# Block products for the first batch's second layer, 64-row value products in early pairs, and a new hand-written order, in a fused attention and feed-forward kernel

## The chip, the cores and the metric

The kernel runs on one core of a Trainium2 chip. The core has TensorE (PE, matrix products into PSUM), VectorE (DVE), ScalarE (ACT), GpSimd (POOL) and SyncE (SP, which here only issues DMAs). The metric is the time of one execution in device microseconds; less is better.

## The reference: what is computed

Cosine attention for 8 batches, 12 heads, 448 positions and 64 dimensions, followed by a feed-forward layer of 768 to 2048 to 768 on all 3584 positions:

```
q_n = q / (norm(q) + 1e-6);  k_n = k / (norm(k) + 1e-6)
attn = softmax(q_n @ k_n.T / tau);  x = attn @ v          # heads side by side: 768 wide
h = x @ w_in;  g = h * clip(h + 3, 0, 6) / 6;  out = g @ w_out
```

Inputs and output are float32; the products run on bf16.

## The kernel before, in words

**Pairs.** The two heads g = 0 and 1 of a batch that are 6 apart are worked on together as one pair; there are HP = 6 pairs in a batch and NP = 48 in all. Items are the query or key halves of two pairs: item j is loaded by `load_qk` (LQ, on SP's queue) into one of the buffers `raws` inside the large tile `big`, squared (`square`, SQ, on DVE, ACT or POOL as its second argument v, a or p says), summed by a DVE `reduce` (RE), turned into inverse norms on ACT (`norms`, NO; with "v" the last steps on DVE), multiplied (`normalise`, NM) and transposed, on PE (`transposes`, TR) in the early items and by DMA (`crossbar`, XD) from item 14 on. `copy_q`, `copy_k`, `copy_k3` (CQ, CK, CS) bring the transposed halves to where the scores read them.

**Attention.** The keys of a pair are taken in four groups: three with 128 keys of each head and a fourth, "M", with the last 64 keys of both heads in one tile, head A in rows 0 to 63 and head B in rows 64 to 127. `scores` (SC, L435 and L438) multiplies keys by queries, mostly in 64 rows of PE, since a head has 64 dimensions; `exps` (EX, L456) exponentiates on ACT; `values` (VA, L478) multiplies by the values, eight matmuls of 65 columns for each group, into the PSUM tile `PV`; the 65th column gives the softmax's sum. `finish_values` (FI) divides on DVE. `back` (BK) or a DMA (`back_crossbar` XB, `back_two` XP) and `copy_x` (CX) make x transposed. In group M the value tile `vx` has zero rows where the other head's keys are, so that 128 rows can be used; from pair FIRST = 18 on the matmuls take only the 64 rows of their own head.

**Feed-forward.** `mm1_unit` (L583) makes 128 of the 2048 hidden values for one batch, in six matmuls of 448 columns, one for each pair of the batch; ACT (`relu`) and DVE (`product`) make g from them. For the second product, positions are taken in tiles of 128; batch 0 has tiles 0 to 2, and its last 64 positions join batch 1. From batch 1 on, tiles are taken in pairs (`PAIRS`) and the product of two tiles with `w_out` is done by seven block products of 8 matmuls (`product_unit`, L756; numbered 1 to 7) from sums of blocks of g (`g_sum`, L734) and of `w_out` (`weight_sums`, L705). The sums y3 and y4 replace blocks of `w_out` in place. ACT copies the products 3, 4, 5 and 2, DVE adds into 1, 6 and 7, POOL makes the three additions of `both` and `rest`. Product 5 goes on in the bank of 3, and 2 in that of 4, once ACT has copied those. A tile without a partner is done by `single_unit` (L836): two units of 16 matmuls, with the sum "e" of g, because `w_out` has been changed. Batch 0 is done by `mm2_unit` (L630) on the unchanged `w_out`, six units of 16 matmuls.

**The order.** Each engine does its instructions in the order in which the program names them. Up to pair 17 that order is written out by hand, token by token, in `PLAN`: the name of an operation, its numbers and its engine. U takes the next unit of `stream` (first products "1" and second products "2", in the sequence `ORDER`); UA and UV do the next waiting finishing step on ACT or DVE. DP.n puts n filler matmuls of zeros (L938, 248 columns) on PE, D.n the same with 512 columns (L933); they keep PE running where it has nothing to do yet. W issues the next weight DMA from POOL's queue, WS is a weight sum, GL copies the 64 leftover positions of a batch. From pair 18 on a loop names the operations; `units`, `TURNS` and `side` say which products and sums go with which pair. Transposed tiles, scores and units share six PSUM banks in turn (`next_bank`) once the start's own banks are closed (OPEN); an operation that gets a bank waits for the reader of its last content.

Of the kernel before, what the change touches and what calls it, by code (L numbers as in the profile page):

```python
# [17 lines left out]
FIRST = 18  # L18
ORDER = "111111111111111111111111111111222222"

PLAN = [
# [42 lines left out]
def kernel(  # L64
# [72 lines left out]
    def raw_before(j):  # L137

        return j - NR if j < 26 else j - NR + 2

    def raw_buffer(j):
        return raws[j % NR if j < 26 else (j - 26) % (NR - 2)]
# [326 lines left out]
    def values(i, g):  # L469
# [4 lines left out]
        for n, name in enumerate(GROUPS[g]):  # L474
            for j in range(4):
                for h in (range(2) if name == "M" else ["AB".index(name[0])]):
                    rows = slice(64 * h, 64 * h + 64) if name == "M" and i >= FIRST else slice(0, 128)
                    nc.tensor.matmul(  # L478
                        pv_out(j, h),
                        at[rows, n, q_cols(i // HP, j)],  # L480
                        vt[rows, 3 + h if name == "M" else 5 * h + int(name[1]), :],
                        start=(name in ("A0", "B0") and j == 0),
                        stop=last,
                        skip_group_check=True,
                    )
# [57 lines left out]
    evac_n = [0]  # L543
# [33 lines left out]
    def mm1_unit(b, fc):  # L577
        needs(*(("CX", i) for i in range(b * HP, (b + 1) * HP)))
        assert len(weights) <= 10 - 2 * (4 * fc // FCN)
        x, g, c0 = xT[b % 2], g_of(b), b % 2 * SR  # L580
        ps, key = bank_of(None, 1)
        for cc in range(CC):
# [3 lines left out]
                x[:, cc, 0:S],  # L586
                start=(cc == 0),
                stop=(cc == CC - 1),
            )
        def relu():  # L590
# [32 lines left out]
    def mm2_unit(b, t, m):  # L623
        assert not weights and ("y4", "y3")[m] not in [x for x, _ in summed]
        complete(b, t)
        g = g_of(b)
        ps, key = bank_of(None, 1)
        cols = slice(m * MH, m * MH + MH)
        for fc in range(FCN):
            nc.tensor.matmul(  # L630
                ps[:, 0:MH],
                g[:, fc, g_cols(b, t)],
                w_out_sb[:, fc, cols],
                start=(fc == 0),
                stop=(fc == FCN - 1),
            )

        def store():
            o = out_tile()
            if on_act:  # L640
                nc.scalar.copy(out=o[:, :], in_=ps[:, 0:MH])
            else:
                nc.vector.tensor_copy(out=o[:, :], in_=ps[:, 0:MH])
            unread[key] = 0
            result(b, t, cols, o)

        evac_n[0] += 1
        on_act = evac_n[0] % 2 == 1
        post["a" if on_act else "v"].append(store)

# [3 lines left out]
    def second(b):  # L654
        assert b % 2 == 0
        return [(mm2_unit, b, t, m) for m in (1, 0) for t in range(3)]
# [7 lines left out]
    PAIRS = [p for b in range(0, B, 2) for p in (((b, 0), (b, 1)), ((b + 1, 3), (b + 1, 0)), ((b + 1, 1), (b + 1, 2)))][1:]  # L664
# [10 lines left out]
    wide_late = [tail(c, MH) for c in range(TAIL, TAIL + 2 * (len(PAIRS) - LOOP) * MH, MH)]  # L675

    def sum_of(n, what):
# [3 lines left out]
        if n < LOOP or n == len(PAIRS) - 1:  # L681
            return gs[what + str(n % 2) if what == "7" else what]
        return late_sums[n % 2][what]

    def d_and_e(n):
        if n < LOOP:
            return wide[n % 2], wide[2]
# [427 lines left out]
```

## Time and profile before

| What | us |
|---|---|
| Median of 3 runs (lowest to highest) | 403.25 (402.74 to 404.51) |
| The profiled execution's own time | 403.12 |
| Its span, from the first to the last instruction | 401.3 |
| PE busy | 393.5 |
| DVE busy | 288.7 |
| ACT busy | 275.4 |
| POOL busy | 238.4 |

The mean granted clock of TensorE was 0.999 of full speed. The span is what the profile divides by; the time of an execution is 1.8 us longer. A line of a group names the source line, engine, operation, output and inputs, then how often it stands and how long one takes. Matmuls are pipelined: one shown with 326 ns lets the next one start after about 160.

### The profile page before, as it was taken

To read this page: it belongs to the slowest core of one execution; us is meant where nothing else is said; L and a number is where in the kernel's file an instruction comes from. 1 tells how busy PE (TensorE), PEld (TensorE's weight loads), DVE (VectorE), ACT (ScalarE), POOL (GpSimd) and SP (SyncE) were. 2 spreads that over 40 slices of the span, in tenths; PEclk is the share of its full clock that TensorE was granted. 3 is DMA by queue.
4 is the path that set the end of the run, shared out by engine and by line. 5 is a ranking of instruction groups with operands and counts; after the bars stand their busy time and mean duration, and the time that the engine had idled before them with its cause. 6 is when DMAs were issued, how large, how long until landed. Compare 5 with 4: busy or idle time off the path is not lost.

```text
span 401.3 us, 9620 instructions
## 1 busy us (share of the span) xinstructions
PE 393.5 (98%) x3691; PEld 235.1 (59%) x3691; DVE 288.7 (72%) x521; ACT 275.4 (69%) x600; POOL 238.4 (59%) x230
## 2 busy tenths in 40 slices
PE   7999999999999999999999999999999999999996
PEld 5666556556665556555555556555555556555563
DVE  7898968779768877677867887697656566644663
ACT  5899889978467687777858769668648755235230
POOL 7799858772554987588475966857665500500070
PEclk9999999999999999999999999999999999999999
DMA  8999999995869559684889658985863423140134
GB/s 289 312 234 238 170 205 280 192 231 143 194 136 238 113 144 207 168 231 110 194 193 204 157 130 158 175 192 140 185 158 71 106 46 68 31 89 20 28 72 99
DMA packets 93166, 63.75 MB, mean 159 GB/s; under 512 B 56128, under 2 KB 93120, under 8 KB 93120
## 3 DMA queue, kind: packets, MB, share of 16 engines
q1 hardware_dynamic: 87408, 56.45, 60.1%
q0 software_dynamic: 5312, 6.29, 9.5%
q8 instruction: 29, 0.48, 0.5%
q10 hardware_dynamic: 400, 0.39, 0.3%
q14 instruction: 17, 0.14, 0.1%
HBM read 45.61 MB, written 11.01 MB: 141 GB/s over the span
## 4 chain that ended last, share of the span: by engine, by line
PE 94%; ACT 3%; DVE 2%; issue 0%
PE M L583 26%; PE M L756 17%; PE PV L478 12%; PE M L438 5%; PE Y L583 5%; PE Z L583 5%; PE Y L756 5%; PE Z L756 4%; PE M L630 3%; PE M L836 3%; ACT at L456 2%; PE PV L938 2%; PE Z L438 2%; PE Y L438 1%; PE Z L836 1%; PE Y L630 1%
## 5 line engine op out<-in xcount | busy, mean ns | idle before, releaser
L583 PE MATMUL M<-xT,w_in_sb 128*128 128x448 bf16 x540 | 113.8, 352 | 0.0
L583 PEld LDWEIGHTS <-w_in_sb 128*128 128x128 bf16 x768 | 72.1, 98 | 63.6 <-issue 3.0
L456 ACT ACTIVATE at<-M 128x448 bf16<-128x448 f32 x193 | 96.2, 568 | 19.0 <-PE Y L438 9.8
L289 POOL TENSOR_TENSOR nrm<-big,r 128x896 bf16<-128x896 f32 (+1 forms) x46 | 76.4, 1666 | 8.1 <-ACT r L279 3.0
L230 POOL TENSOR_TENSOR big<-big 128x896 f32<-128x896 f32 (+4 forms) x46 | 71.8, 1564 | 14.3 <-DMA big<-in_k_dram 6.2
L598 DVE SCALAR_TENSOR_TENSOR gT<-u,M 128x448 bf16<-128x448 bf16 x80 | 49.5, 618 | 38.3 <-ACT u L592 37.6
L592 ACT ACTIVATE u<-M,bias 128x448 bf16<-128x448 f32 x90 | 58.8, 653 | 25.7 <-PE M L583 25.0
L478 PEld LDWEIGHTS <-at 128*128 128x128 bf16 (+1 forms) x1536 | 54.2, 97 | 20.2 <-issue 11.8
L478 PE MATMUL PV<-vx,at 128*128 128x65 bf16 (+1 forms) x1536 | 62.9, 193 | 0.0
L395 POOL COPY km<-tT 64x128 bf16<-64x128 bf16 x34 | 14.7, 433 | 67.0 <-DMA tT<-nrm 35.1
L242 DVE TENSOR_REDUCE n<-big 128x14 f32<-128x896 f32 (+1 forms) x50 | 51.6, 1041 | 0.7 <-POOL big L230 0.4
L785 POOL TENSOR_TENSOR big<-big 128x384 f32<-128x384 f32 x11 | 11.9, 1084 | 54.5 <-ACT big L804 54.4
L756 PEld LDWEIGHTS <-gT 128*128 128x128 bf16 x288 | 27.9, 98 | 19.6
L499 DVE TENSOR_TENSOR on<-PV,rc 128x512 bf16<-128x512 f32 x48 | 33.2, 692 | 1.7
L456 ACT ACTIVATE at<-Z 128x448 bf16<-128x448 f32 x52 | 29.3, 563 | 4.4 <-PE Z L438 2.3
L756 PE MATMUL M<-w_out_sb,gT 128*128 128x384 bf16 x176 | 32.2, 326 | 0.0
L438 PE MATMUL M<-tT,kz 64*128 64x448 bf16 (+1 forms) x173 | 31.5, 351 | 0.3 <-ACT at L456 0.3
L456 ACT ACTIVATE at<-Y 128x448 bf16<-128x448 f32 x49 | 27.7, 565 | 5.7 <-PE Z L438 5.7
L756 PEld LDWEIGHTS <-gs 128*128 128x128 bf16 x224 | 21.5, 98 | 14.7 <-DVE gs L734 0.3
L308 POOL CAST vx<-big 128x512 bf16<-128x512 f32 x37 | 27.5, 748 | 0.8 <-DMA big<-in_v_dram 0.7
L756 PE MATMUL M<-w_sum,gs 128*128 128x384 bf16 (+1 forms) x160 | 27.7, 318 | 0.0
L583 PE MATMUL Y<-xT,w_in_sb 128*128 128x448 bf16 x114 | 24.7, 352 | 0.0
(134 smaller groups left out, 565.9 us busy)
## 6 DMA issues: line engine op xcount, KB each, us to landing
big<-in_k_dram SPq DMA_DIRECT2D x24, 448.0 KB, 5.1
big<-in_q_dram SPq DMA_DIRECT2D x24, 448.0 KB, 4.3
out_dram<-o SPq DMA_DIRECT2D x107, 96.0 KB, 2.2
big<-in_v_dram SPq DMA_DIRECT2D x48, 128.0 KB, 4.5
big<-in_v_dram SPq DMA_DIRECT2D x48, 96.0 KB, 4.5
w_in_sb<-in_moe_w_in_dram POOLq DMA_DIRECT2D x8, 384.0 KB, 6.5
w_out_sb<-in_moe_w_out_dram POOLq DMA_DIRECT2D x4, 768.0 KB, 10.7
tT<-nrm SPq DMA_TRANSPOSE x34, 3.0
```

Of the source, the lines that this page charges most:

```text
L230: engines[e].tensor_tensor(out=o, in0=i, in1=i, op=ALU.mult)
L242: nc.vector.tensor_reduce(out=n2_and_r[0][:, d % 2, j % 2, c], in_=sq[:, :, :, :].rearrange("p g c d -> p (g c) d")[:, c, :], axis=AX.X, o ...
L289: engines[e].tensor_tensor(out=nrm[:, :, g, :].rearrange("p c g d -> p g c d"), in0=raw_of[j][:, g, :, :], in1=n2_and_r[2][:, d % 2, j % 2, :]
L308: (engines[e].copy if e == "a" else engines[e].tensor_copy)(out=o, in_=f)
L438: nc.tensor.matmul(o, ks, qt[rows], start=True, stop=True)
L456: nc.scalar.activation(out=o, in_=x, func=AF.Exp, scale=inv_tau)
L478: nc.tensor.matmul(pv_out(j, h), at[rows, n, q_cols(i // HP, j)], vt[rows, 3 + h if name == "M" else 5 * h + int(name[1]), :], start=(name ...
L499: nc.vector.tensor_tensor(out=on[:, :, :, :].rearrange("p j h d -> p h j d"), in0=pv4[:, :, :, 0:D], in1=rc[:, :, :].to_broadcast([128, 2, ...
L583: nc.tensor.matmul(ps[:, 0:S], w_in_sb[:, cc, fc * 128 : (fc + 1) * 128], x[:, cc, 0:S], start=(cc == 0), stop=(cc == CC - 1),)
L592: nc.scalar.activation(out=u[:, :], in_=ps[:, 0:S], func=AF.Relu, bias=half_bias, scale=1.0 / 6.0)
L598: nc.vector.scalar_tensor_tensor(out=g[:, fc, c0 : c0 + S], in0=u[:, :], scalar=1.0, in1=ps[:, 0:S], op0=ALU.min, op1=ALU.mult,)
L756: nc.tensor.matmul(m, lhs[:, c, :], rhs[:, c, c0 : c0 + width], start=(base is None and c == 0), stop=(c == KC - 1), skip_group_check=True,)
```

## The change

- Batch 0's tiles 0 and 1 become a pair of their own, numbered -1, done by seven block products in the sequence 3, 4, 5, 2, 1, 6, 7; tile 2 becomes a single (s0.0, s0.1). `mm2_unit` is gone. For it the plan names five sums of g (GS.6, 2, 7, 5, 1), the sum "e" for the single, two POOL steps (UP) and all of the weight sums; the last half of y4 leaves the loop's `side[18]`.
- `values` takes a third argument: with ".t" in the plan, group M of an early pair is done in 64 rows. Thirteen of the first 17 pairs have it: 0, 1, 3, 6, 7 and 9 to 16.
- The first four first products of batch 0 are cut into pieces of 2, 2 and 1 matmuls (UH), named as the transposed pairs become ready, and a rest that U does.
- The order of nearly all of `PLAN` is new: the first transposition stands behind 40 fillers where it stood behind 50, the second behind 53 where it was 60; fillers of 248 columns number 96 where they were 90, those of 512 columns 2 where it was 1. Squares, copies and casts go to other engines: 4 casts of values on DVE where there were 9, 4 on ACT where there were 2, 40 on POOL where there were 37. Item 20 is loaded later, into another buffer (`raw_buffer`).

The diff without the plan, cut to its core:

```diff
-ORDER = "111111111111111111111111111111222222"
+ORDER = "1" * 30 + "2" * 9
...
     def raw_buffer(j):
-        return raws[j % NR if j < 26 else (j - 26) % (NR - 2)]
+        return raws[5 if j == 20 else j % NR if j < 26 else (j - 26) % (NR - 2)]
...
-    def values(i, g):
+    def values(i, g, by_halves=None):
...
-                    rows = slice(64 * h, 64 * h + 64) if name == "M" and i >= FIRST else slice(0, 128)
+                    rows = slice(64 * h, 64 * h + 64) if name == "M" and (by_halves or i >= FIRST) else slice(0, 128)
...
+    CUTS = (0, 2, 4, 5)
+    open_units = {}
+
+    def mm1_piece(b, fc, c0, c1, bank=None):
+
+        needs(*(("CX", b * HP + c) for c in range(c0, c1)))
+        assert len(weights) <= 10 - 2 * (4 * fc // FCN)
+        if c0 == 0:
+            open_units[b, fc] = *bank_of(bank, 1), 0
+        ps, key, n = open_units[b, fc]
+        assert n == c0
+        for cc in range(c0, c1):
             nc.tensor.matmul(
                 ps[:, 0:S],
                 w_in_sb[:, cc, fc * 128 : (fc + 1) * 128],
-                x[:, cc, 0:S],
+                xT[b % 2][:, cc, 0:S],
                 start=(cc == 0),
                 stop=(cc == CC - 1),
+                skip_group_check=True,
             )
+        open_units[b, fc] = ps, key, c1
...
     def second(b):
-        assert b % 2 == 0
-        return [(mm2_unit, b, t, m) for m in (1, 0) for t in range(3)]
+        return products(" ".join(f"{x}.{b - 1}" for x in "3452167") + f" s{b}.0 s{b}.1")
...
-    PAIRS = [p for b in range(0, B, 2) for p in (((b, 0), (b, 1)), ((b + 1, 3), (b + 1, 0)), ((b + 1, 1), (b + 1, 2)))][1:]
+    PAIRS = dict(
+        enumerate((p for b in range(0, B, 2) for p in (((b, 0), (b, 1)), ((b + 1, 3), (b + 1, 0)), ((b + 1, 1), (b + 1, 2)))), -1)
+    )
...
     def d_and_e(n):
+        if n < 0:
+            return tuple(big[:, RAW + c : RAW + c + MH] for c in (0, MH))
...
     side = {
-        18: [(weight_sums, "y4", KC // 2, KC // 2)], 19: sums(0, "62"), 20: sums(0, "1"),
+        19: sums(0, "62"), 20: sums(0, "1"),
```

The part of the new plan around batch 0's second products (each line of the plan is a string):

```
"SC.15.1 U EX.15.0 EX.15.1 FI.13 VA.14.0 VA.14.1 VA.14.2 VA.14.3.t UV SC.15.2 U SC.15.3 WS.1.1 UA UA WS.6.1 UV",
"WS.y3.1 FI.14 LV.8 EX.15.2 WS.y3.0 XD.17 U U EX.15.3 UA VA.15.0 XP.12 WS.7.1 WS.y4.0 WS.y4.1 CS.16.v VC.18.a",
"LV.10 GS.5 GS.1 CK.17.a VA.15.1 CK.16.a VA.15.2 UA U U UA UA U UA U UV UV UV UP GL.0 XD.18 SC.16.0 VA.15.3.t",
```

More of the change, by code (lines that the diff above doesn't have):

```diff
@@ L137, in raw_before @@
     def raw_before(j):
-        return j - NR if j < 26 else j - NR + 2
+        return 19 if j == 20 else j - NR if j < 26 else j - NR + 2
     def raw_buffer(j):
-        return raws[j % NR if j < 26 else (j - 26) % (NR - 2)]
+        return raws[5 if j == 20 else j % NR if j < 26 else (j - 26) % (NR - 2)]
     sqs = [item(NR + i) for i in range(2)]
@@ L541, in back_two @@
             issued.update((("BK", x), ("CX", x)))
-    evac_n = [0]
     post = {"a": [], "v": [], "p": []}
@@ L575, in g_left @@
         left_done.add(b)
-    def mm1_unit(b, fc):
-        needs(*(("CX", i) for i in range(b * HP, (b + 1) * HP)))
+    CUTS = (0, 2, 4, 5)
+    open_units = {}
+    def mm1_piece(b, fc, c0, c1, bank=None):
+        needs(*(("CX", b * HP + c) for c in range(c0, c1)))
         assert len(weights) <= 10 - 2 * (4 * fc // FCN)
-        x, g, c0 = xT[b % 2], g_of(b), b % 2 * SR
-        ps, key = bank_of(None, 1)
-        for cc in range(CC):
+        if c0 == 0:
[3 more added lines that the diff above has]
+        for cc in range(c0, c1):
             nc.tensor.matmul(
@@ L585, in mm1_unit @@
                 w_in_sb[:, cc, fc * 128 : (fc + 1) * 128],
-                x[:, cc, 0:S],
+                xT[b % 2][:, cc, 0:S],
                 start=(cc == 0),
                 stop=(cc == CC - 1),
+                skip_group_check=True,
             )
+        open_units[b, fc] = ps, key, c1
+    def mm1_unit(b, fc):
+        mm1_piece(b, fc, open_units[b, fc][2] if (b, fc) in open_units else 0, CC)
+        ps, key, _ = open_units.pop((b, fc))
+        g, c0 = g_of(b), b % 2 * SR
         def relu():
@@ L621, in out_tile @@
         return sb.tile([128, MH], FP32, name="o", tag="o", bufs=4)
[L623 to L649, printed above, removed]
     def firsts(b, *fcs):
@@ L654, in second @@
     def second(b):
-        assert b % 2 == 0
-        return [(mm2_unit, b, t, m) for m in (1, 0) for t in range(3)]
+        return products(" ".join(f"{x}.{b - 1}" for x in "3452167") + f" s{b}.0 s{b}.1")
     LEFT, RIGHT = slice(0, MH), slice(MH, 2 * MH)
-    PAIRS = [p for b in range(0, B, 2) for p in (((b, 0), (b, 1)), ((b + 1, 3), (b + 1, 0)), ((b + 1, 1), (b + 1, 2)))][1:]
+    PAIRS = dict(
+        enumerate((p for b in range(0, B, 2) for p in (((b, 0), (b, 1)), ((b + 1, 3), (b + 1, 0)), ((b + 1, 1), (b + 1, 2)))), -1)
+    )
+    LAST = max(PAIRS)
     LOOP = 8
@@ L674 @@
     wide = [big[:, c : c + MH] for c in range(0, 3 * MH, MH)]
-    wide_late = [tail(c, MH) for c in range(TAIL, TAIL + 2 * (len(PAIRS) - LOOP) * MH, MH)]
+    wide_late = [tail(c, MH) for c in range(TAIL, TAIL + 2 * (LAST + 1 - LOOP) * MH, MH)]
     def sum_of(n, what):
@@ L680, in sum_of @@
             return gs["1"] if n < B - 2 else late_sums[1]["e"]
-        if n < LOOP or n == len(PAIRS) - 1:
+        if n < LOOP or n == LAST:
             return gs[what + str(n % 2) if what == "7" else what]
@@ L743, in product_unit @@
         base = None if apart else {"2": "4", "5": "3", "6": "1"}.get(name)
+        if n < 0:
+            needs(("NM", 13))
+            assert base is None or (n, base) in ready
         if base is None:
@@ L876 @@
     }
-    APART = {(n, y) for n in range(len(PAIRS)) for x, y in (("5a", "3"), ("2a", "4")) if f"{x}.{n}" in " ".join(TURNS.values()).split()}
+    APART = {(n, y) for n in PAIRS for x, y in (("5a", "3"), ("2a", "4")) if f"{x}.{n}" in " ".join(TURNS.values()).split()}
     side = {
-        18: [(weight_sums, "y4", KC // 2, KC // 2)], 19: sums(0, "62"), 20: sums(0, "1"),
+        19: sums(0, "62"), 20: sums(0, "1"),
         21: sums(1, "75"), 22: sums(1, "621"),
@@ L965 @@
         "NM": normalise, "VC": vcast, "TR": transposes, "XD": crossbar, "XB": back_crossbar, "XP": back_two, "CQ": copy_q, "CK": copy_k, "CS": copy_k3, "SC": scores,
-        "EX": exps, "VA": values, "FI": finish_values, "BK": back, "CX": copy_x, "U": unit, "UA": lambda: finish_units("a"), "UV": lambda: finish_units("v"),
+        "EX": exps, "VA": values, "FI": finish_values, "BK": back, "CX": copy_x, "U": unit, "UH": lambda n, k, bank=None: mm1_piece(0, n, CUTS[k], CUTS[k + 1], bank), "UA": lambda: finish_units("a"), "UV": lambda: finish_units("v"), "UP": lambda: finish_units("p"), "GS": lambda x, *n: g_sum(*((0, "e") if x == "e" else (-1, str(x)))),
         "GL": g_left, "WS": lambda x, *h: weight_sums(str(x), *((h[0] * KC // 2, KC // 2) if h else (0, KC))), "UU": whole_units, "D": busy, "DP": busy_pv, "OPEN": open_ring,
```

76 rows, old and new, of the table PLAN are left out of this document.

## The prediction, written before the changed kernel was run

> **What bounds the kernel now.** I read the page's busy rows first, then the waits of TensorE (PE), then the timelines of the start, then the stretches of 5 and 10 us.
>
> ```profile
> PE 393.5 (98%) x3691; PEld 235.1 (59%) x3691; DVE 288.7 (72%) x521; ACT 275.4 (69%) x600; POOL 238.4 (59%) x230
> ```
>
> PE is busy for 98% of the span and the other engines are far below it. Its waits:
>
> ```profile
> PE PV L938 <- DVE xT L986: 2.5, 1, 2.5
> PE SC L438 <- DVE tT L357: 0.5, 2, 0.4
> PE SC L438 <- ACT at L456: 0.3, 1, 0.3
> PE M L438 <- ACT at L456: 0.3, 1, 0.3
> ```
>
> Columns: total us, times, longest. So time is saved here almost only where PE's own instructions get fewer or shorter. Busy PE is not PE at its rate, however: a matmul's shown 326 ns overlaps the next one. I therefore use distances from start to start, from the chain in order of time and the PE timeline:
>
> ```profile
> 2.48 8.13 PE PV L938 x50
> 10.99 1.06 PE PV L938 x10
> 94.55 2.60 PE M L630 x16
> 118.52 1.30 PE M L756 x8
> 38.84 0.65 PE L478 MATMUL PV<-vx,at 128*128 128x65 bf16 x16
> 39.42 0.36 PE L438 MATMUL Y<-tT,kz 64*128 64x448 bf16 x1
> 120.96 0.63 PE L478 MATMUL PV<-vx,at 128*128 128x65 bf16 x16
> 121.43 0.35 PE L438 MATMUL Z<-tT,kz 64*128 64x448 bf16 x1
> 122.09 0.66 PE L478 MATMUL PV<-vx,at 128*128 128x65 bf16 x16
> 122.59 0.32 PE L756 MATMUL Z<-w_out_sb,gT 128*128 128x384 bf16 x1
> ```
>
> A second-product matmul of 384 columns takes 2.60/16 = 162 ns, in L630 and in L756 alike. A filler matmul (L938, 248 columns) takes 106 ns, after a slow start: the first 50 take 163 each. Sixteen value matmuls of full rows take 0.50 us before full-row work (122.09 to 122.59) and 0.58 before the scores, which use 64 rows (38.84 to 39.42): a change between 128 and 64 rows costs about 0.09. At 120.96 eight of the sixteen already are 64-row ones, and the scores start after 0.47: halving the rows of eight matmuls saves 0.58 - 0.47 = 0.11.
>
> The start is the one part that PE does not bound alone:
>
> ```profile
> 15.00:20.00 5.00, 4.84 (x67) 3.23 (x64) 4.83 (x12) 4.97 (x10) 3.96 (x4) 1.00 1.04 359
> 25.00:30.00 5.00, 4.72 (x86) 3.18 (x85) 4.90 (x12) 4.97 (x9) 5.00 (x5) 1.00 1.13 204
> 90.00:100.00 10.00, 10.00 (x114) 6.18 (x113) 9.07 (x14) 8.33 (x19) 2.48 (x3) 1.00 0.57 145
> ```
>
> Columns after the stretch: its length, PE, weight loads, DVE, ACT, POOL, granted clock. From 15 to 30 us ACT and DVE are as full as PE, and the fillers hide how much PE really has to do. From 90 to 100 DVE is nearly full, POOL is not.
>
> **The change, part by part.** The counts come from the two programs' orders, engine by engine.
>
> (1) Second products of batch 0: 6 tiles of 16 matmuls (96) become 7 block products of 8 and 2 singles of 16 (88). 8 x 0.162 = **-1.30 us** on PE.
>
> (2) Fillers: 90 become 96, and a second 512-column one (L933, next start 0.23 later) comes in: 6 x 0.106 + 0.23 = **+0.86**.
>
> (3) Thirteen early pairs take their last keys in 64 rows: 13 x 0.11 = **-1.46** (with 0.112). The order holds 153 changes of row mode where it held 145, so 8 x 0.096 (the same distances, 125 against 29 ns) = **+0.77**. The row for the saving is the late pairs' own, so I take it as it is; most of the 13 groups stand beside scores, which pay a change of mode anyway. The Trainium skill, TensorEngine Tiling (Array Packing), section Key Properties, says against this part that changing the tiling mode drains TensorE; the trace agrees (0.09 us each time). Rival (d) is what that rule would do at worst.
>
> PE's own rows: -1.30 + 0.86 - 1.46 + 0.77 = **-1.13**.
>
> (4) Batch 0's first products are cut into pieces of 2, 2 and 1 of their 6 matmuls. Same matmuls, no cost; they fill PE while the last transposes arrive.
>
> (5) The start. Against the sum of its rows, PE's starts lag 5.1 us at the first transposition (10.44: 2.5 of wait and the slow fillers) and 7.9 at 41 us: 2.8 us are lost there. 0.4 of it is the wait of the first scores on the DVE copy. In the new order ten fillers fewer stand before the first transposition and seven before the second, so PE and with it DVE's copy come earlier; adding DVE's rows up to that copy, it ends at about 12.3 us and PE arrives at 12.5, so I drop the 0.4. Then exps: they take 0.80 us for two banks and 0.42 for one, from start to start. Summing ACT's queue, squares, norm steps and copies at their rows included, from the first exps to those of pair 7 gives 26.6 us before and 26.7 after; PE's rows between the same scores give 25.4 and 26.0. So PE must wait for ACT 1.1 us before and 0.6 after: -0.5. DVE's queue, summed in the same way up to each pair's division, is 0.9 us late at worst before and on time after. I take **-0.9**; the bounds are -2.8 (all of the loss goes) and +1.1 (the new order costs further waits as long as all those for scores of before, 0.5 + 0.3 + 0.3).
>
> (6) What DVE must do earlier. All weight sums now stand before batch 0's products, where they stood beside and behind them, with five sums of g in between and a sixth before the singles. Rows of before: a half weight sum 0.87 to 0.95, a sum of g 0.68. Following DVE's queue from about 76 us of the span: 11 us of such sums and 10 of its usual work lie in the 21 us until product 4, so nothing is spare. y3 ends some 0.5 before product 3 needs it, y4 0.5 after product 4 could start. What is queued behind that waiting matmul on PE is all the rest, so it counts in full: **+0.7** with small waits of banks. Bounds: 0 (DVE has run ahead) and +3.5 (rival b, two lost sums).
>
> (7) Hidden: POOL gets 3 additions of 1.0 us, beside 2.5 us of work in 90:100, ACT two more copies of 0.48 in a stretch where it has 1.7 of 10 free; if that cover is gone, a product's bank comes free half a microsecond later. The load of item 20 (key or query half of pairs 20 and 21) moves on SP's queue from 69 to about 104 us, behind normalise 19; its transposition then waits on SP until about 115 us, with a few output DMAs behind it, and its scores come some 20 us later. The loop from pair 18 on is the same but for one weight sum less (0.95 to 1.35 of DVE); PE has no wait there now, so it gains nothing.
>
> Sum: -1.13 - 0.9 + 0.7 = -1.3. The profiled execution took 403.12 us (span 401.3 and 1.8 around it), 0.13 below the median of 403.25: **401.8 us**.
>
> **Rivals.**
>
> (a) The start loses its waits altogether and y4 is in time: -1.13 - 2.0 + 0 gives 400.0. For it: every queue I summed has more room in the new order. Against: ACT is still 0.6 us short, and DVE's sums are tight. From -0.9 less y4's wait on it passes the 0.5% line.
>
> (b) The sums under POOL: slower. A sum of g of 1,024 elements takes
>
> ```profile
> L734 DVE TENSOR_TENSOR gs<-gT x26: 679/682/2170, 120.8 to 339.0; 128x1024 bf16<-128x1024 bf16 x26
> ```
>
> so 0.68 mostly, but up to 2.17. The long ones (131.5, 147.3, 235.4 us and others) lie under a normalise or square of POOL, though some short ones do as well. In the new order the sums 6 and 2 of g and half of weight sum 7 stand where POOL's queue holds three normalises in a row (1.65 us each). Each can lose up to 1.5 us; DVE has nothing spare, so product 4 and the next division wait by so much. Two lost sums: 403.12 - 1.13 - 0.9 + 3.5 = 404.6. It is slower by 0.5% from three on: with 0.5 + 3 x 1.5 = 5.0 of wait it is 406.1. Against: later POOL is nearly empty in the new order (casts moved to ACT), so the y sums run free.
>
> (c) No gain: ACT alone sets the start, so fewer PE instructions there only become waits (the four 64-row groups before 41 us, 0.44, are worth nothing), and y4's wait stays: -1.13 + 0.44 + 0.7 = 0.0, 403.1. For it: ACT's 4.97 of 5.00. Against: the cheaper matmuls after 41 us, and all of part 1, lie where only PE is full.
>
> (d) The 64 rows do not pay, because each group pays two changes of row mode of its own: 13 x 2 x 0.096 = 2.5 against the 1.46 saved, +1.0 where part 3 had -0.7, so 403.5. The counted changes speak against it.
>
> **Chances.** A measurement of this kernel can tell about 0.5% (2.0 us) from no change. Forecast 401.8: 0.45, with 0.05 of it beyond the line of 401.2; (a) 0.28; (b) 0.14, of which 0.09 beyond 405.3; (c) 0.08; (d) 0.05. Faster by over 0.5%: 0.33; within 0.5%: 0.40 + 0.05 + 0.08 + 0.05 = 0.58; slower: 0.09. The range goes from (a) with the whole bound of part 5 (403.12 - 1.13 - 2.8 = 399.2) to (b) with two lost sums, 404.6.
>
> **What would show it.** Right: PE's first scores start without a wait on DVE, at about 12.5 us; the loop's first scores stand about 1.3 us earlier than before and the distance stays to the end; products of batch 0 take 1.30 per eight; a wait of PE of about 0.5 us in front of product 4 (the L751 line) on a DVE weight sum. Wrong: weight sums or sums of g on DVE that take over 1 us between 80 and 98 us (b), more waits on exps between 15 and 41 us (c), a value group of the last keys whose next start comes after 0.2 us (d).

## The result, and the profile after

The changed kernel takes 409.90 us (median of 6 runs, 409.55 to 411.46); the kernel before, beside it, took 403.74 (402.74 to 404.71). The ratio is 1.0169, with an interval of 1.0145 to 1.0193: slower, where 401.8 was forecast and 404.6 was the upper end of the range. The profiled execution took 409.8 us with a span of 407.8; its mean granted clock was 0.990.

The page's busy rows and its row of granted clock:

```profile
PE 394.7 (97%) x3690; PEld 233.4 (57%) x3690; DVE 295.5 (72%) x528; ACT 278.9 (68%) x604; POOL 236.5 (58%) x235
...
PEclk9999999699999999999999999999999999999999
```

One slice of forty, from 71 to 82 us, has a clock of 0.6, and DVE is busy for 6.8 us more than before. TensorE's waits (total us, times, longest) name the place:

```profile
PE Z L441 <- DVE kz L360: 4.5, 1, 4.5
PE PV L933 <- DVE xT L981: 2.5, 1, 2.5
PE SC L441 <- DVE tT L360: 1.4, 1, 1.4
```

The 2.5 at the very start stood in before too. The 1.4 of the first scores stands where 0.4 stood, and the 4.5 is new: the scores of pair 12 wait for a key copy of DVE. DVE's timeline there (start, duration, line, operation, output, inputs):

```profile
65.40 7.10 DVE L233 TENSOR_TENSOR big<-big 128x128 f32<-128x128 f32 x1
72.42 0.76 DVE L360 COPY kz<-M 64x64 bf16<-64x64 bf16 x3
```

The key copy stands behind a square of only 128 elements that lasts 7.10 us. It is the last seventh of item 16's square (`SQ.16.v.6.1` in the plan), which POOL did before. POOL's timeline under it:

```profile
64.01 1.69 POOL L233 TENSOR_TENSOR big<-big 128x896 f32<-128x896 f32 x1
65.63 1.16 POOL L311 CAST vx<-big 128x512 bf16<-128x512 f32 x2
66.76 1.46 POOL L233 TENSOR_TENSOR big<-big 128x768 f32<-128x768 f32 x1
68.17 0.81 POOL L921 DMA_DIRECT2D w_out_sb<-in_moe_w_out_dram  x1
69.00 3.34 POOL L292 TENSOR_TENSOR nrm<-big,r 128x896 bf16<-128x896 f32 x2
```

POOL has no gap from 64.01 to 72.34, and DVE's square ends 0.16 us after POOL's last instruction. TensorE's timeline shows what follows:

```profile
66.95 1.30 PE L591 MATMUL Y<-xT,w_in_sb 128*128 128x448 bf16 x6
68.09 0.65 PE L481 MATMUL PV<-vx,at 128*128 128x65 bf16 x16
73.23 0.55 PE L441 MATMUL Z<-tT,kz 64*128 64x448 bf16 x1 [4.49 <-DVE kz L360]
...
74.97 2.40 PE L591 MATMUL M<-xT,w_in_sb 128*128 128x448 bf16 x6
```

After the wait the same six matmuls take 2.40 us where they took 1.30; the stretch from 73 to 79 us has a granted clock of 0.53. The Trainium skill, TensorE: Matmul & The Clock Gate, section Part 1, says that an idle window of about 3.4 us sets the clock back to half; the trace agrees (4.5 us of idleness, then 0.53).

**Where the time went.** As in the prediction I set PE's starts against the sum of its rows before them, and call the difference the lag. The sum is 386.98 us after and 388.16 before.

| Lag of PE, us | before | after |
|---|---|---|
| at the first scores | 5.6 | 6.2 |
| near 35 us | 7.5 | 7.3 |
| near 60 us | 8.0 | 8.3 |
| near 79 us | 8.3 | 15.9 |
| at the end | 9.1 | 16.7 |

So the rows gave -1.18, the start about nothing by 35 us, and the 19 us from 60 to 79 cost 7.3 more than before. The sum, -1.18 + 7.6 = 6.4, is the difference of the spans, 6.5.

### The profile page after: what moved, and what is told of

It is laid out like the page before. It is cut to its first block, busy times and chain, and to the rows that moved or that the text cites. A ratio compares the mean times of both kernels' runs of the same rounds, so it can differ in the third digit from the quotient of the medians.

```text
span 407.8 us, 9652 instructions
## 1 busy us (share of the span) xinstructions
PE 394.7 (97%) x3690; PEld 233.4 (57%) x3690; DVE 295.5 (72%) x528; ACT 278.9 (68%) x604; POOL 236.5 (58%) x235
## 4 chain that ended last, share of the span: by engine, by line
PE 85%; DVE 6%; ACT 3%; issue 2%; POOL 2%; DMA 1%; SPq 0%; POOLq 0%; ACTq 0%
PE M L591 22%; PE M L751 19%; PE PV L481 11%; PE Z L591 6%; PE M L441 5%; PE Y L591 5%; PE Y L751 4%; PE Z L751 4%; PE M L831 3%; DVE big L233 2%; PE Y L441 2%; ACT at L459 2%; DVE gT L614 1%; PE Y L831 1%; PE Z L441 1%
## 5 line engine op out<-in xcount | busy, mean ns | idle before, releaser
L591 PE MATMUL M<-xT,w_in_sb 128*128 128x448 bf16 x510 | 110.3, 356 | 0.1
L292 POOL TENSOR_TENSOR nrm<-big,r 128x896 bf16<-128x896 f32 (+1 forms) x48 | 79.4, 1659 | 13.7 <-ACT r L282 5.7
L233 POOL TENSOR_TENSOR big<-big 128x896 f32<-128x896 f32 (+5 forms) x43 | 65.3, 1519 | 21.8 <-DVE n L245 6.3
L608 ACT ACTIVATE u<-M,bias 128x448 bf16<-128x448 f32 x85 | 55.3, 653 | 24.2 <-PE M L591 23.6
L614 DVE SCALAR_TENSOR_TENSOR gT<-u,M 128x448 bf16<-128x448 bf16 x75 | 45.9, 618 | 29.9 <-ACT u L608 29.1
L751 PEld LDWEIGHTS <-gT 128*128 128x128 bf16 x320 | 30.9, 98 | 21.6 <-DVE gT L726 0.2
L751 PE MATMUL M<-w_out_sb,gT 128*128 128x384 bf16 x192 | 35.0, 326 | 0.0
L751 PE MATMUL M<-w_sum,gs 128*128 128x384 bf16 (+1 forms) x192 | 33.5, 319 | 0.0
L751 PEld LDWEIGHTS <-gs 128*128 128x128 bf16 x248 | 23.9, 98 | 16.2 <-issue 0.2
L591 PE MATMUL Z<-xT,w_in_sb 128*128 128x448 bf16 x144 | 31.3, 352 | 0.0
```

The source lines that it names most:

```text
L233: engines[e].tensor_tensor(out=o, in0=i, in1=i, op=ALU.mult)
L292: engines[e].tensor_tensor(out=nrm[:, :, g, :].rearrange("p c g d -> p g c d"), in0=raw_of[j][:, g, :, :], in1=n2_and_r[2][:, d % 2, j % 2, :]
L591: nc.tensor.matmul(ps[:, 0:S], w_in_sb[:, cc, fc * 128 : (fc + 1) * 128], xT[b % 2][:, cc, 0:S], start=(cc == 0), stop=(cc == CC - 1), ski ...
L608: nc.scalar.activation(out=u[:, :], in_=ps[:, 0:S], func=AF.Relu, bias=half_bias, scale=1.0 / 6.0)
L614: nc.vector.scalar_tensor_tensor(out=g[:, fc, c0 : c0 + S], in0=u[:, :], scalar=1.0, in1=ps[:, 0:S], op0=ALU.min, op1=ALU.mult,)
L751: nc.tensor.matmul(m, lhs[:, c, :], rhs[:, c, c0 : c0 + width], start=(base is None and c == 0), stop=(c == KC - 1), skip_group_check=True,)
```

## The experiments

My theory after the result: the square waits on DVE for POOL's whole run because both need the same way into SBUF, and everything else follows from it. Rivals: the key copy is late for another reason, the clock alone costs the time, or the new start does. Every kernel below was compared with the kernel before on its own chip (medians 403.0 to 403.4).

### 1. Is it the square, and is it its two inputs?

On ACT instead:

```diff
-SQ.16.v.6.1
+SQ.16.a.6.1
```

> The changed kernel with one token undone: the last seventh of item 16's squares (128 elements) goes to ACT instead of DVE. Theory P (port): on DVE this square, with two inputs in SBUF, stood 7.1 us because POOL's instructions followed each other without a gap; PE's 4.6 us wait for the key copy behind it, and the 2.6 us that its matmuls then lose at half the clock, both go: 409.9 - 7.2 = 402.7 us, and the granted clock is 0.99 or more in every stretch. Theory D (data): the square waited for its load or its buffer; then ACT waits for the same, the exps behind it are late by some 4 us, and the time stays at 408 to 410 us.

Measured: 404.09 us (402.47 to 408.44), ratio 1.0024 (0.9991 to 1.0058, which is 1.4 us either way). So about 5.8 of the 6.2 us lost are this one instruction's doing, and the median is 1.4 above the 402.7 expected here.

In its place on DVE, with one input (a reduction over an axis of one, so an absolute value):

```diff
+        elif e == "v" and j == 16:
+            nc.vector.tensor_reduce(
+                out=o, in_=i.rearrange("p g c (d x) -> p g c d x", x=1), axis=AX.X, op=ALU.max, apply_absolute_value=True
+            )
```

> The changed kernel with the DVE square replaced in its place by an operation with one input, a maximum over one element that gives absolute values instead of squares for that seventh of item 16 (so one seventh of the squares of item 16's norms is wrong). Same tile read and written, same elements, same place in DVE's order. Theory P: it takes 0.2 to 0.3 us under the same POOL run, PE does not wait, 402.7 us. Theory D: it takes about 7 us like the square, 409.9 us.

Measured: 404.28 us, ratio 1.0017 (0.9992 to 1.0042), and in DVE's timeline

```profile
67.25 0.23 DVE L233 TENSOR_REDUCE big<-big 128x128 f32<-128x128 f32 x1
```

Same place, same elements, same run of POOL over it: 0.23 us for 7.10. The operation is another one too, but `tensor_tensor` as such does not wait for POOL. The changed kernel's divisions are `tensor_tensor` with one of their two inputs in PSUM. They take 0.69 us in all 48 cases, 26 of them begun while POOL worked (ns, lowest, median and highest, then first and last start):

```profile
L502 DVE TENSOR_TENSOR on<-PV,rc x48: 691/691/693, 19.8 to 344.8; 128x512 bf16<-128x512 f32 x48
```

So it is the second input from SBUF. The Trainium skill, SBUF — State Buffer, section Who interferes with whom, states this: a DVE instruction with two inputs in SBUF shares a read port with GpSimd, `tensor_reduce` does not, and the one that comes second waits for the other's whole instruction. The trace agrees on the kind and not on the length: the square waited through all that was left of seven instructions, not through one.

### 2. Would another place do, and how much of it is the clock?

The square behind the key copies of pairs 12 and 13:

```diff
-NO.7.v W SQ.16.v.6.1 SC.11.2
+NO.7.v W SC.11.2
...
-CS.13.v EX.11.3
+CS.13.v SQ.16.v.6.1 EX.11.3
```

> The changed kernel with the same square on DVE, moved behind the four key copies of pairs 12 and 13. Theory P: the scores of pair 12 no longer wait; the square starts some 3 us later and still ends with POOL's run of instructions, so it takes 2 to 4 us instead of 7, and holds up only DVE's next steps: 403 to 404.5 us. Theory L (the instruction is long by itself, whenever it starts): 7 us again, now in front of the finishing step of pair 11 and the products, and the time stays above 407 us.

Measured: 409.56 us, ratio 1.0153 (1.0134 to 1.0171). The time missed my expectation; DVE's line tells why:

```profile
67.66 4.99 DVE L233 TENSOR_TENSOR big<-big 128x128 f32<-128x128 f32 x1
```

It starts 2.3 us later and ends at the same moment, 72.65, with POOL's run (72.49). The copies were free, but a finishing step (L614) now stood behind the square and held a PSUM bank: PE waited 3.7 us for that. Moving the instruction doesn't shorten it; it changes who is behind it.

Forty fillers on PE in front of the scores that wait:

```diff
-CX.8.a SC.12.0
+CX.8.a DP.40 SC.12.0
```

> The changed kernel with 40 filler matmuls (4.2 us) in front of the scores that wait 4.6 us for the key copy. The wait itself stays. Theory C (clock): the matmuls after the wait took 0.36 to 0.38 us instead of 0.19 because PE had stood idle; fillers keep it busy, so these 2.6 us go and the wait for the copy shrinks to some 0.5: 409.9 - 2.6 = 407.3 us. Rival: the slow matmuls have another cause (weights still arriving, banks being read); then they stay slow and the time is 409.9 or a little more.

Measured: 409.08 us, ratio 1.0169 (1.0109 to 1.0229). The clock stays at 1.000 and the six matmuls take 1.29 again, yet the span is only 0.7 shorter (407.1 against 407.8; lag 16.1 with the 4.24 us of fillers counted, against 16.7). PE now waits in three short pieces (0.2 to 0.3 each) for DVE, which is 7 us behind. So the half clock is real, but here it mostly lies over a delay that DVE would have set anyway: it is not a term to be added in full.

### 3. Which operations wait for the whole run?

Other two-input operations of DVE meet POOL in these traces and get their turn at the end of one of its instructions (sums of 1,024 and 1,536 elements, 1.0 to 2.4 us in all). What sets this square apart? Two different operands:

```diff
+        elif e == "v" and j == 16:
+            nc.vector.tensor_tensor(out=o, in0=sqs[1][:, :, 5:6, :], in1=sqs[1][:, :, 6:7, :], op=ALU.mult)
```

> In place of the last square of item 16 DVE multiplies two different parts of item 17's squares, 128 elements f32, at the same place (one seventh of item 16's sum of squares is replaced by that product). If the 7 us came from one operand read twice, the product is handed over at the end of one of POOL's instructions and takes 0.3 to 2.5 us, and the time is that of the kernel with the square on ACT, 403 to 405. If it is any short two-input f32 operation that waits for POOL's whole run, it takes 5 to 7 us and the time is 409 to 410.

Measured, in one execution: 6.77 us, 408.95. One operand read twice is not the cause. Longer squares, POOL's part cut by as much (four sevenths on DVE here; two and three in the other kernels):

```diff
-SQ.16.p.0.6 VA.10.0
+SQ.16.p.0.3 VA.10.0
...
-SQ.16.v.6.1 SC.11.2
+SQ.16.v.3.4 SC.11.2
```

> DVE squares four sevenths of item 16 (512 elements f32) where it squared one (128), and POOL squares three where it squared six; nothing is left out. If it was the small size that lost against POOL's run, the longer square is handed over at the end of one POOL instruction, takes 0.6 to 2.5 us, and the time is 403 to 405. If any f32 square waits for POOL's whole run, it ends with that run, which is 1.0 to 1.5 us shorter now: 4 to 6 us of duration, and the time is 407 to 409.

> The changed kernel with DVE squaring two sevenths of item 16 (256 elements) where it squared one (128); POOL squares five where it squared six. If size decides with a limit between 128 and 256 elements, the square is handed over at the end of one POOL instruction: 0.4 to 2.0 us, time 403 to 405.5. If the limit lies above 256, it lasts till the end of POOL's run: 5 to 7 us, time 408 to 410.

> The changed kernel with DVE squaring three sevenths of item 16 (384 elements; POOL four). 128 and 256 elements waited till the end of POOL's run, 512 did not. If a size between 256 and 384 decides, the square takes 0.5 to 2.0 us and the time is 403 to 405.5; if the limit lies above 384 or it was not the size, it lasts 4.5 to 7 us and the time is 407 to 410.

Measured with 512, 256 and 384 elements, one execution each: 1.83, 7.06 and 6.78 us; 405.53, 413.71 and 413.30 us. In the last two another 3 to 4 us were lost at the start, where a load came late (section 5). DVE's line with 384 elements, then DVE's and POOL's with 512:

```profile
68.89 6.78 DVE L233 TENSOR_TENSOR big<-big 128x384 f32<-128x384 f32 x1
```
```profile
66.90 1.83 DVE L233 TENSOR_TENSOR big<-big 128x512 f32<-128x512 f32 x1
```
```profile
66.96 1.16 POOL L311 CAST vx<-big 128x512 bf16<-128x512 f32 x2
68.09 1.32 POOL L233 TENSOR_TENSOR big<-big 128x384 f32<-128x384 f32 x1
```

Both were issued just before POOL's two casts. The long one ran at the casts' end, 68.1, and POOL's square was the one that waited: 1.32 us, where 384 elements take 0.83 elsewhere. The 384 ones got no turn before POOL's run ended. The changed kernel shows one more case, a DVE normalise of 448 elements with both inputs in SBUF, and POOL's two instructions beside it:

```profile
44.48 1.32 DVE L292 TENSOR_TENSOR nrm<-big,r 128x448 bf16<-128x448 f32 x1
```
```profile
44.46 0.84 POOL L233 TENSOR_TENSOR big<-big 128x384 f32<-128x384 f32 x1
45.24 1.03 POOL L311 CAST vx<-big 128x512 bf16<-128x512 f32 x1
```

It got in at the square's end, 45.30, and the cast behind it took 1.03 where 0.61 is usual. That looks like a size, with the limit between 384 and 448 elements. But 256, 384 and 512 were tried in one execution each, beside the 512 POOL's own square was shorter too, and a normalise is not a square, so size is the likelier reading and not shown.

The same 128 elements at another place:

```diff
-SQ.15.p.4.3
+SQ.15.p.4.2 SQ.15.v.6.1
```

> A square of 128 elements on DVE at another place: the last seventh of item 15, at about 58 us, where POOL also works without a gap (the item 16 square is on ACT, and the two copies of the start are exchanged). If a short two-input operation waits for the whole run of POOL, it lasts over 3 us here too, and the wait shows at PE; time 405 to 410. If the first place was a special case, it lasts at most 2 us, and the time is 403.5 to 405.

Measured, in one execution: 0.23 us, 403.28. It tells nothing of the special case: at 57.3 us POOL was idle, and its run began only after the square. It gives the price alone, 0.23.

### 4. Is what remains the start?

Two copies read one transposed bank and write one tile: DVE's queries of pair 0 and ACT's of pair 1. In the new order ACT's was given out first:

```diff
-TR.0.Z CQ.1.a CQ.0.v
+TR.0.Z CQ.0.v CQ.1.a
```

The new kernel's lines, ACT, then DVE:

```profile
11.60 1.03 ACT L231 ACTIVATE big<-big 128x384 f32<-128x384 f32 x2
12.54 0.51 ACT L358 COPY tT<-Z 128x448 bf16<-128x448 bf16 x1
```
```profile
13.08 0.39 DVE L360 COPY tT<-Z 128x448 bf16<-128x448 bf16 x1 [0.77 <-ACT tT L358]
```

DVE waits for ACT's copy, and that stands behind two squares. All kernels from here on have the square on ACT and, but where it is said, this exchange.

> The changed kernel with the last square of item 16 on ACT and, at the start, DVE's query copy of pair 0 given out ahead of ACT's query copy of pair 1. Theory (the two copies read one transposed bank and write one tile, so the later one given out waits for the other; DVE's copy of pair 0 stood behind ACT's of pair 1, which stood behind two squares of 1.03 us): DVE's copy starts at about 12.3 us instead of 13.1, the wait of the first scores falls from 1.4 to at most 0.5, and the time is about 1.0 us below that of the kernel with the square on ACT alone (404.1): 402.5 to 403.3, a ratio to before of 0.998 to 1.000. Rival (ACT's queue sets the start, and the wait only moves): the first scores start earlier, PE then waits as long in front of the scores of pairs 1 or 2, and the time stays at 404.1, a ratio of 1.002.

Measured: 404.16 us, ratio 1.0018 (0.9991 to 1.0045). DVE's copy starts at 12.25 and the first scores wait 0.6 instead of 1.4, as expected. But by 28 us the lag is 6.7, as in the changed kernel: the wait only moves, as the rival has it. Its reason, ACT's queue, does not hold in this trace. What was won lasts to 26 us, and then ACT and POOL both stand idle for the load of item 9:

```profile
25.25 0.63 ACT L231 ACTIVATE big<-big 128x512 f32<-128x512 f32 x1 [0.71 <-DMA big<-in_k_dram]
```
```profile
25.30 0.83 POOL L233 TENSOR_TENSOR big<-big 128x384 f32<-128x384 f32 x1 [0.70 <-DMA big<-in_k_dram]
```

In the changed kernel the same two squares start at 25.33 and 25.29, with no wait in front. So a start that is ahead by 0.9 us is held there by a load.

The order of before up to the scores of pair 6, then the new one, with the key copies of the next experiment:

> The same as the kernel with the key copies later, but with the order of before from the start to the scores of pair 6 (with three of its value groups in 64 rows), so that only the part behind about 40 us is new. The sum of PE's rows is 386.3 us, 1.85 below before. If the new start is what cost the rest, and the late part keeps its gain, the time is 401.0 to 401.8, a ratio of 0.994 to 0.997. If the start of the new order costs nothing against that of before, the time differs from the kernel with the new start by the rows alone, 0.7 us. If the late part has still more waits of its own, it stays at 403 or above.

Measured: 403.74 us, ratio 1.0016 (0.9998 to 1.0034), while the same late part with the new start took 403.59. So the new start is not what keeps the time up, as far as these intervals (0.7 and 1.1 us either way) can tell.

### 5. The parts by themselves, and the waits that are next

The 64-row groups alone, put into the kernel before:

```diff
-VA.3.3
+VA.3.3.t
```

(and twelve more)

> The kernel before with one part of the change alone: thirteen early pairs take their value products of the last keys in 64 rows. By the prediction's prices (0.11 saved in each group, 0.096 for each of ten more changes of row mode): 13 x 0.11 - 10 x 0.096 = -0.5 us, a ratio of 0.9988, hardly to be told from no change. Rival (d), each group pays two changes of its own: 13 x 2 x 0.096 - 1.46 = +1.0 us, a ratio of 1.0026. In the trace the eight halved matmuls of a last group take 0.47 less 0.36 us, not the time of full rows.

Measured: 402.65 us (401.93 to 403.78), ratio 0.9983 (0.9968 to 0.9998): -0.7 us (-1.3 to -0.1) for the expected -0.5, and rival (d) is out. The last group of pair 3, with its distance to the scores, in this kernel and in before:

```profile
39.08 0.63 PE L478 MATMUL PV<-vx,at 128*128 128x65 bf16 x16
39.55 0.35 PE L438 MATMUL M<-tT,kz 64*128 64x448 bf16 x2
```
```profile
39.92 0.65 PE L478 MATMUL PV<-vx,at 128*128 128x65 bf16 x16
40.51 0.36 PE L438 MATMUL M<-tT,kz 64*128 64x448 bf16 x2
```

0.47 us instead of 0.59. This part alone is the only version tried whose interval lies below the kernel before, and only just.

In the kernel with the exchanged copies PE waited 1.0 us at 107 us behind a DVE key copy that waited 2.7 us for item 16's transposition on SP's queue. Those copies later:

```diff
-GS.5 GS.1 CK.17.a VA.15.1 CK.16.a VA.15.2
+GS.5 GS.1 VA.15.1 VA.15.2
...
-GL.0 XD.18
+GL.0 CK.17.a CK.16.a XD.18
```

> The kernel with the square on ACT and the two copies of the start exchanged, and in addition DVE's key copies of pairs 16 and 17 given out behind batch 0's last additions, where they stood ahead of them. Theory (once the square is gone, the next thing late is item 16's transposition on SP's queue: DVE's copy waited 2.7 us for it, and the additions behind it freed a product's bank 1.0 us late, 1.5 with what followed): the wait of 1.0 at 107 us goes and the time falls by 1.0 to 1.5, to 402.7 to 403.2, a ratio to before of 0.997 to 1.000. Rival: the copies are needed as soon by the scores of pair 16, so the wait only moves there, and the time stays at 404.2 (1.002).

Measured: 403.59 us (402.16 to 407.1), ratio 1.0024 (0.9998 to 1.0051). The wait at 107 is gone. Two others stand in this profile, which the one without the edit doesn't have; the first is POOL at the start:

```profile
8.67 0.83 POOL L233 TENSOR_TENSOR big<-big 128x384 f32<-128x384 f32 x1 [2.81 <-DMA big<-in_k_dram]
```

POOL's half of the first normalise stands behind this square, which waits for item 3's load; PE waits 1.1 us at the first transposition. In 6 of the 12 profiles with the new start up to here this square began at 8.4 to 9.0 us and PE waited 0.5 to 1.9; in the others it began at 6.8 to 7.1, and PE waited in one of them (0.6). Before, both halves were on DVE and ten more fillers stood in front. The half back on DVE:

```diff
-NM.1.p.0
+NM.1.v.0
```

> The kernel with the key copies later, and the first item's second half normalised on DVE, as before, instead of on POOL, where it stands behind a square that waits for the load of item 3. In the profiles that load's square started at 6.8 us in some executions and at 8.7 to 9.0 in others, and in the latter PE waited 0.5 to 1.3 for POOL's half at the first transposition. Theory: with the half on DVE this wait is gone (0 to 0.2 us), the first transposition starts by 9.3 us in the profile, and the median falls by 0.5 to 1.0 from 403.6, to 402.6 to 403.1, a ratio of 0.998 to 1.000, with fewer executions over 405. Rival: the half on DVE pushes the reductions behind it by 0.6, and the wait only moves to the first scores: 403.6 again (1.002).

Measured: 403.28 us (402.07 to 406.24), ratio 1.0009 (0.9987 to 1.0031); no wait at the first transposition, and the lag near 35 us is 6.9, the lowest with the new start up to here. The first scores wait 1.1 us, though, where they waited 0.6 with the copies exchanged alone, so a part of the wait did move there, as the rival has it. The load was early in this profile, so the late case is not seen, and the two times can't be told apart.

The second wait, 1.0 us at 86, is my rival (b). DVE's and POOL's lines, with the key copies later:

```profile
83.49 2.26 DVE L697 TENSOR_TENSOR w_sum<-w_out_sb 128x1536 bf16<-128x1536 bf16 x1
```
```profile
83.25 4.05 POOL L292 TENSOR_TENSOR nrm<-big,r 128x896 bf16<-128x896 f32 x2
```

Half a weight sum takes 2.26 where it takes 0.95 free. With the exchanged copies alone the same sum came 1.6 us earlier, ahead of this run of normalises, and took 0.95. It is a race, decided by where the two queues happen to be. Moved later, and moved earlier (with the new start and with the old):

```diff
-CS.14.v UV UV WS.7.0 U EX.13.3 U CK.14.a U UA UA UV SQ.21.a.0.4
+CS.14.v UV UV U EX.13.3 U CK.14.a U UA UA UV WS.7.0 SQ.21.a.0.4
```

```diff
-UV U WS.6.0 EX.13.1
+UV U WS.6.0 WS.7.0 EX.13.1
...
-CS.14.v UV UV WS.7.0 U EX.13.3
+CS.14.v UV UV U EX.13.3
```

> The same, and in addition the first half of weight sum 7 (DVE, two inputs) behind the key copy of pair 14 and the finishing steps that stood behind it. In two profiles this sum met POOL's run of two normalises at 83 us and took 1.7 and 2.3 us for 0.95, the key copy behind it came late and PE waited 1.0 to 1.4 with what followed; in others DVE was first and nothing waited. Theory: the sum no longer holds the copy, so the wait on it at 86 us is gone, and the median falls by up to 0.7 against the kernel without this edit, to 402.0 to 402.9 (0.997 to 0.999). Rival: the sum loses as much at the new place, and holds up a division or a finishing step instead: no difference.

> The kernel with the first normalise on DVE (403.3), and the first half of weight sum 7 right behind that of sum 6, at about 80 us, where it starts before POOL's run of normalises does and not into it. Theory (this sum loses 0.8 to 1.4 us to POOL in about half of the executions, and in all of them where it stood later): it takes 0.95 in the profile, nothing waits at 83 to 87 us, and the median falls by 0.5 to 1.0, to 402.3 to 402.8, a ratio to before of 0.997 to 0.999. Rival: the key copy and the division that now stand behind it come 0.95 later and hold PE instead: 403.3 or above.

> The kernel with the order of before up to the scores of pair 6 (403.7), with the same move of weight sum 7. Theory: the executions of 404 and more, which make about half of that kernel's, go, and the median falls to 402.0 to 402.6 (0.996 to 0.998): the rows' 1.85 less about 0.5 of small waits and 0.2 outside the span. Rival as above: 403.7 or more.

Measured: 404.69 us (404.17 to 405.93), 1.0043 (1.0030 to 1.0056); 404.47, 1.0033 (1.0013 to 1.0054); 403.49, 1.0007 (0.9990 to 1.0024). The first two are slower than before by their intervals. Later, the sum takes 2.35. Earlier, it takes 0.95 as expected, and the next two-input operation meets the normalises in its stead:

```profile
84.00 2.00 DVE L726 TENSOR_TENSOR gs<-gT 128x1024 bf16<-128x1024 bf16 x1
```

A sum of g, 2.00 for 0.68, and PE waits 0.7 behind it. Both theories of the last two failed: with these sums so close together, some one of them meets POOL, and moving one hands the loss to the next.

## Why the prediction was wrong

- **The failed step is one that is not in it.** The part-by-part account follows DVE's queue up to 41 us and again from about 76; the square that the new order gives to DVE at 65 us appears nowhere, and so at nothing, where even its bare price is 0.2. It cost about 5.8 us by the experiment on ACT. Rival (b) names the mechanism, a two-input operation of DVE under POOL, but looks for it among the sums at 80 to 98 us, prices it by the sums' longest row, 2.17, and counts up to three. The row was no bound, since no row of before could show this price: its one short square on DVE (192 elements at 4.3 us, 0.36) began while POOL was idle. Under POOL's run a short one took 7.10.
- **Parts (1) to (3) held.** PE's rows fell by 1.18, forecast 1.13; that is the same kind of sum, and no run showed all of it in the time. What the runs showed: eight second-product matmuls of batch 0 take 1.30 us from start to start, and the 64-row groups alone gave -0.7 (-1.3 to -0.1).
- **Part (5) was wrong in its first term.** The first scores were to lose a wait of 0.4 and got one of 1.4. I had summed DVE's own rows up to the end of the copy of pair 0 (12.3 us; with the copies exchanged it runs from 12.25 to 12.6), and not asked what else the copy waits for: ACT's copy from the same bank. The other term, -0.5, came: from the first scores to 35 us the lag grew by 1.1 us where it grew by 1.9 before. So -0.9 came to -0.2 by 35 us. What I left out altogether are the loads: one holds POOL's square and with it the first normalise, another holds ACT and POOL at 25 us when the start is ahead. That ACT alone sets the start, as rival (c) had it, no trace shows.
- **Part (6) was wrong in the changed kernel, right in kind without the square.** y4's wait of 0.7 did not come: product 4 waited for nothing. With the 7-us delay gone, one of the sums loses 0.8 to 1.4 us in 5 of the 11 profiles of kernels without the slow square; in the six with it none does. That is rival (b)'s mechanism, at less than its 1.5 us for each sum.
- **Part (7), hidden, held in the changed kernel.** Nothing on PE waited for SP's queue there; in a kernel that came there earlier, item 16's transposition on SP cost 1.0 to 1.5 us.
- **The best version of the whole change, 403.28, is no faster than before.** In its profiled execution (403.01, span 401.2; before 403.12 and 401.3): rows -1.18, start -0.6, and from 35 us on +1.7 (the lag grows by 3.3 against 1.6), together -0.1. Not all of these 1.7 us are traced to single waits; which of them could still go is open.

## What to carry to other kernels

When an order is searched anew, list every two-input DVE operation that changed engine or place, and set each beside POOL's queue. A short one can cost the time to the end of POOL's unbroken run (here 5 to 7 us), a long one the time to the end of one POOL instruction (here up to 1.5); an instruction with one input in SBUF, or ACT, was the way out here. When two engines copy out of one bank into one tile, count for the second copy the later of both queues, and count the loads as a queue too. And a gain in PE's rows is only worth what the next-late engine leaves of it: undo the one large loss first, then look again, since the next waits stand under it.

## What the runs showed of the hardware that was not expected

- A DVE product of 128, 256 or 384 f32 elements with two inputs in SBUF waited 4.99 to 7.10 us, to the end of POOL's unbroken run in each of the six profiles, and then took 0.15 to 0.42. It was not let in between two of POOL's instructions, while the normalises of 448, the square of 512 and the sums of 1,024 and 1,536 elements were.
- An execution takes 1.8 us more than its span with the kernel before and with the 64-row groups alone (means of 1.79 to 1.81), and 1.95 to 2.07 (means of four executions or more) with every kernel that has the new late part. What these 0.2 us are, the traces don't show.
